# Low bits of two weight pairs on ScalarE, and another order of the first part, in a fused attention and feed-forward kernel

## The chip, the cores and the metric

The kernel runs on one core of a Trainium2 chip. The metric is the device time of one execution in microseconds (us); lower is better. TensorE multiplies matrices, VectorE and ScalarE do elementwise work, POOL (GpSimd) does masks and small powers, and SP issues the DMA transfers from a queue that it takes in order. Each engine takes its own instructions in program order and waits for others by semaphores.

## The reference

Gated linear attention over 4 batches of 8 heads, 768 positions and 48 numbers a head, then a gated feed-forward layer behind an RMS norm, then a second one with squared ReLU:

```python
f = 1 / (1 + exp(-f_logit))
for t in range(S):
    state = f[:, :, t, :, None] * state + einsum('bhd,bhe->bhde', k[:, :, t], v[:, :, t])
    y[:, :, t] = einsum('bhd,bhde->bhe', q[:, :, t], state)
x = y.transpose(0, 2, 1, 3).reshape(B * S, H * D)
...
xn = x / sqrt(mean(x * x) + 1e-6) * rms_g
x = (silu(xn @ w_gate) * (xn @ w_val)) @ w_out          # 384 -> 1536 -> 384
...
out = relu(x @ w_in) ** 2 @ w_out2                      # 384 -> 2048 -> 384
```

The weights come as 64-bit floats; the rest is 32-bit.

## The kernel before

**Units and groups.** Attention is cut into 24 units: 6 chunks of 128 positions by 4 batches. Unit `u` is chunk `u // 4` of batch `u % 4`. Four units form a group of 512 rows for the first feed-forward layer; there are six groups. A group runs twelve steps: `G` and `V` are the gate and value products of step `f` (nine matmuls of 512 columns each, since every 32-bit operand is split in a high and a low part), `si` is the silu of the gate on ScalarE, `vs` the product with the value on VectorE, `hh` and `hl` split the result in high and low, and `O` multiplies it into three accumulator banks. `G` has one PSUM bank and `V` one, so the next `G` waits for the silu of the last, and the next `V` for its product.

**Weights.** The first layer's weights come in 18 pairs (`g0 v0`, `o0 g1`, `v1 o1`, ...) of 768 64-bit numbers a partition, tile `raw` with two 32-bit words for each number. A pair is made 32-bit in pieces: `wl` loads it; `ws` takes the high word as a float and scales it (ScalarE, line 568); `wb` shifts the result by 3 bits (VectorE, line 572) and ors the low word's top 3 bits in (line 579); `wc` ors the sign in (line 589); `wh` and `wz` split the number in a high part (ScalarE, line 626) and a low one (VectorE, line 630). `raw` and `m` have two buffers each, so a later load waits for an earlier pair.

**The first part.** Everything up to the end of group 0 is written out by hand in the string `FIRST`. Each word is a piece and its index, and the pieces are issued in that order; every engine's own order follows from it. `lr`, `lf`, `lk`, `lq`, `lv` load parts of a unit 0 to 3, and `ld` loads all of a later unit (gates `ff`, then `qk`, then `v`). `gr` and `gf` are the sigmoids of the gates (for units from 4 on `gr` is both, lines 296 and 297), `sb` and `sa` the scans, `mk` and `mq` the products with `k` and `q`, `sc` the scores, `ca` and `cb` the copies of the scores out of PSUM, `pa` and `pb` the masks on POOL, `kt` and `kc` the transposed keys, `y` the attention, `kv` and `st` the state, `no`, `pw`, `nr` the norm, `xt`, `xh`, `xl` the input tiles of the first layer. `du` issues dummy matmuls. `G0` needs `xl` of units 0 to 3.

**The seam.** The last word of group 0's work is `O11`. It also copies the three accumulators out of PSUM (ScalarE, line 936) and has SP store each (line 937). Then the loop `phase1` begins with group 1, whose pieces are placed by a planner. Its first segment has, on ScalarE and in this order, the gates of unit 8, a small copy of their end (which waits for VectorE's scan of them) and the silu of group 1's step 0. From there to the end the order doesn't depend on `FIRST`.

Of the kernel before, what the change touches and what calls it, by code (L numbers as in the profile page):

```python
# [8 lines left out]
F32 = mybir.dt.float32  # L9
F32R = mybir.dt.float32r  # L10
BF16 = mybir.dt.bfloat16
I32 = mybir.dt.int32
AF = mybir.ActivationFunctionType
ALU = mybir.AluOpType
PSUM = bass.MemoryType.PSUM

P = 128
# [12 lines left out]


FIRST = """
lr1 lr3 gr1 lf1 lr0 gf1 sb1 gr0 lk1 lf0 lq0 gf0 lq1 sa1 mk1 lr2 sb0 mq1 gr2 lk0 wl3 lf2 gr3 kt1 sa0 lk2 sc1 lv1
kc1 cb1 ca1 ws3 pa1 lf3 lv0 mk0 mq0 sb2 gf2 sc0 wb3 sa2 ca0 mk2 pb1 y1 pa0 ld4 kv1 cb0 sb3 lq2 pb0 gf3 no1 kt0
kc0 y0 wc3 lk3 st1 no0 sa3 mk3 kt2 pw1 kv0 pw0 nr1 xt1 wl0 mq2 gr4 lq3 lv2 st0 wh3 nr0 kc2 du6 sc2 lv3 ws0 xh1
sb4 wl1 mq3 sc3 cb2 wz3 pb2 ca2 wb0 cb3 pa2 ca3 pb3 sa4 xl1 ld5 xt0 wc0 xh0 kv2 y2 xl0 du10 kt3 mk4 ws1 no2 wh0
wl2 pa3 y3 pw2 nr2 no3 wb1 kc3 xt2 kv3 mq4 st2 pw3 nr3 xt3 xh2 xh3 wz0 ws2 wc1 xl2 xl3 sc4 wh1 en0 wl4 kt4 gr5
G0 si0 wb2 wz1 wc2 wh2 cb4 V0 sb5 wz2 ws4 pb4 vs0 G1 st3 en4 de4 wb4 si1 ca4 hh0 mk5 pa4 kc4 V1 wc4 sa5 wl8 hl0
G2 y4 ws8 vs1 wh4 wl5 kt5 no4 kv4 wz4 si2 wb8 O0 G3 mq5 wc8 pw4 hh1 ws5 wh8 en3 wb5 V2 wc5 wl6 st4 nr4 wh5 wz8
hl1 vs2 ws6 wl7 wz5 ld6 sc5 wb6 si3 kc5 ws7 O1 hh2 wc6 ca5 V3 cb5 wh6 hl2 pa5 wb7 gr6 pb5 wz6 wc7 xt4 wl9 O2 kv5  # L40
sb6 vs3 de5 G4 ws9 wb9 si4 wh7 xh4 y5 V4 wl10 wz7 hh3 G5 wc9 hl3 ws10 en1 no5 vs4 wb10 mk6 de6 pw5 wc10 wh9 O3
en5 wl11 si5 hh4 wz9 hl4 ld7 nr5 sa6 V5 ws11 vs5 wl12 xl4 G6 si6 wb11 wh10 wz10 V6 wc11 vs6 hh5 ws12 wb12 en6
wh11 wz11 wl15 wc12 wh12 kt6 st5 hl5 ws15 O4 G7 hh6 V7 gr7 si7 mq6 O5 wl13 wz12 hl6 wb15 kc6 sc6 mb6 O6 xt5 ws13
vs7 wc15 wh15 G8 wb13 hh7 en2 sb7 wz15 si8 hl7 wl14 xh5 wc13 V8 ma6 ws14 vs8 wh13 wl16 G10 y6 wb14 sa7 wc14 V10
no6 si10 wz13 wl17 O7 hh8 pw6 wh14 wz14 xl5 G9 mk7 mq7 nr6 xt6 ws16 vs10 sc7 hl8 ma7 mb7 V9 xh6 kv6 si9 de7 wb16
y7 vs9 ws17 wc16 O8 hh9 wh16 xl6 hl9 en7 no7 kt7 kc7 wb17 wz16 O9 pw7 wc17 nr7 ld8 st6 wh17 xt7 hh10 xh7 G11
wz17 hl10 V11 si11 O10 xl7 vs11 hh11 kv7 hl11 st7 O11
"""


def exact_path(tc, qk, ff, vT, rms_g, out, w1_order, w2_order, raw_load, to_f32, f64):
# [9 lines left out]
    with ExitStack() as st:  # L61
# [12 lines left out]
        with tc.For_i(0, B, 1) as b, tc.For_i(0, NPAIR, 1) as a, tc.For_i(0, D // EG, 1) as g:  # L74
            bs, as_, gs = bass.ds(b, 1), bass.ds(a, 1), bass.ds(g, 1)

            def load(src, nm):
                t = sp.tile([P, NCH, C], F32, tag=nm, name=nm)
                nc.sync.dma_start(t, src.rearrange("o u p c t -> (o u p) c t"))
                return t.rearrange("p c t -> p (c t)")  # L80

            qt, kt = load(qkb[bs, as_, 0], "xq"), load(qkb[bs, as_, 2], "xk")
            ft = load(fb[bs, as_, 0, :, :, 1:], "xf")
            nc.scalar.activation(ft, ft, AF.Sigmoid)
            fr = cp.tile([P, EG, S], F32, name="x_fr")
# [28 lines left out]
    with ExitStack() as st:  # L114
# [25 lines left out]
        with tc.For_i(0, B * NCH, 1) as i:  # L140
# [3 lines left out]
            rs = sp.tile([P, 1], F32, tag="zrs", name="zrs")  # L144
            nc.scalar.activation(sq, x, AF.Square, accum_out=rs)
            nc.gpsimd.tensor_scalar(rs, rs, 1.0 / DM, EPS, op0=ALU.mult, op1=ALU.add)
# [17 lines left out]
            for f in range(F1):  # L164
                gp, vp = proj(("g", f), xt, "zg"), proj(("v", f), xt, "zv")
                h = sp.tile([P, C], F32, tag="zh", name=f"zh{f}")
                nc.scalar.activation(h, gp, AF.Sigmoid)
                nc.vector.tensor_mul(h, h, gp)
# [9 lines left out]
            for f in range(F2):  # L178
                hp = proj(("a", f), x3, "zg" if f % 2 else "zv")
                r = sp.tile([P, C], F32, tag="zh", name=f"zr{f}")  # L180
                nc.scalar.activation(r, hp, AF.Relu)
                nc.vector.tensor_mul(r, r, r)
# [7 lines left out]
def tile_linear_attention_moe(  # L190
# [11 lines left out]
    nc = tc.nc  # L202
# [4 lines left out]
    def pool(name, stack=main, **kw):  # L207
        return stack.enter_context(tc.tile_pool(name=name, **kw))

    ps = pool("ps", bufs=1, space=PSUM)  # L210
    cp = pool("const", bufs=1)
# [16 lines left out]
    seed = cp.tile([P, NPAIR, C + 1], F32, name="seed")  # L228
    neghalf = cp.tile([P, 1], F32, name="neghalf")
    half = cp.tile([P, 1], F32, name="half")  # L230
    epsT = cp.tile([P, 1], F32, name="epsT")
    ends = cp.tile([P, NCH * B, NPAIR], F32, name="ends")
    gT = cp.tile([P, KT], F32, name="gT")
# [3 lines left out]
    def constants():  # L237
        nc.gpsimd.memset(half, 0.5)
        nc.gpsimd.memset(mask, 1.0)
        nc.gpsimd.affine_select(  # L240
            out=mask, in_=mask, compare_op=ALU.is_ge, fill=0.0,
            base=-(C - 1), pattern=[[1, C]], channel_multiplier=1,
        )
        nc.gpsimd.memset(floor, A_MIN)
        nc.gpsimd.memset(floor[:, :, 0:1], 1.0)
        nc.gpsimd.memset(seed, 0.0)
        make_identity(nc, ident)
        nc.gpsimd.memset(neghalf, -0.5)
        nc.gpsimd.memset(epsT, EPS)
        for st in state:  # L250
            nc.gpsimd.memset(st, 0.0)
# [43 lines left out]
    def sig(x):  # L295
        nc.scalar.activation(x, x, AF.Tanh, scale=0.5)
        nc.scalar.activation(x, x, AF.Identity, bias=half, scale=0.5)

# [255 lines left out]
    f64 = w1.dtype != F32  # L554
    raws = {}

    def raw_load(pool, pair):
        src = w1[w1_order.index(pair)] if pair in w1_order else w2[w2_order.index(pair)]
        if f64:
            raw = pool.tile([P, 2 * DM, 2], I32, tag="raw", name="raw")  # L560
            nc.sync.dma_start(raw.rearrange("p a b -> p (a b)"), src.bitcast(I32))
        else:
# [7 lines left out]
    def to_f32_shift(m, raw):  # L570
        mi = m.bitcast(I32)
        nc.vector.tensor_scalar(
            mi, mi, 3, 0x7FFFFFF8,
            op0=ALU.logical_shift_left, op1=ALU.bitwise_and,
        )

    def to_f32_or(m, raw):
        mi = m.bitcast(I32)
        nc.vector.scalar_tensor_tensor(
            mi, raw[:, :, 0], 29, mi, op0=ALU.logical_shift_right, op1=ALU.bitwise_or,  # L580
        )

    def to_f32_low(m, raw):
        to_f32_shift(m, raw)
        to_f32_or(m, raw)

    def to_f32_sign(m, raw):
        mi = m.bitcast(I32)
        nc.vector.scalar_tensor_tensor(
            mi, raw[:, :, 1], -2 ** 31, mi, op0=ALU.bitwise_and, op1=ALU.bitwise_or,  # L590
        )

    def to_f32_bits(m, raw):
        to_f32_low(m, raw)
        to_f32_sign(m, raw)
# [8 lines left out]
    def wscale(pair):  # L604
        if f64:
            m = rp.tile([P, 2 * DM], F32, tag="m", name="m", bufs=2)
            to_f32_scale(m, raws[pair][0])
            raws[pair][1] = m

    def wbits_low(pair):  # L610
        if f64:
            to_f32_low(raws[pair][1], raws[pair][0])

    def wbits_sign(pair):
        if f64:
            to_f32_sign(raws[pair][1], raws[pair][0])

    def whigh(pair):
# [15 lines left out]
    def w2_half(key):  # L634
        n, f = key
        e = DM * (2 if f64 else 1)
        o = "ab".index(n) * e
        src = w2[f].bitcast(I32) if f64 else w2[f]
        return src[:, o:o + e]
# [104 lines left out]
    wz = mask.bitcast(BF16)  # L744
# [8 lines left out]
    def prologue():  # L753
        nc.sync.dma_start(gT, rms_g.rearrange("(k p) -> p k", p=P))
        for u in range(UG):
            unit_tiles(u)
        constants()
        dense(12)
# [200 lines left out]
    def piece(kind, i):  # L959
# [21 lines left out]
        ld=load_unit, sb=scan_b, en=keep_end, sa=scan_a, mk=mul_k, mq=mul_q, sc=scores, kt=ktrans, kc=kcopy,  # L981
        y=attend, kv=kv, de=decay, st=state_add, no=norm, pw=power, nr=norm2, xt=xtrans, xh=xhigh, xl=xlow,
    )
    pair_piece = dict(wl=wload, ws=wscale, wb=wbits_low, wc=wbits_sign, wh=whigh, wz=wlow)

    def step_piece(kind, gi, f):
        nm = f"{gi}_{f}"
# [467 lines left out]
```

## Time and profile before

| | |
|---|---|
| time, median of 3 runs | 934.64 us (934.61 to 936.6) |
| time of the profiled execution | 936.63 us |
| its span, first to last instruction | 934.8 us |
| mean granted clock of TensorE | 0.993 |
| busy: TensorE, VectorE, ScalarE, POOL | 98%, 68%, 52%, 4% |

A time is that of the whole execution; the span leaves out what lies around the first and the last instruction. Starts in the profile count from the span's start. TensorE is the fullest engine by far, so a change elsewhere counts only where TensorE waits for it.

### The profile page before, as it was taken

What the parts mean: (1) busy time and instruction counts of PE and PEld (TensorE: products, weight loads), DVE (VectorE), ACT (ScalarE), POOL (GpSimd) and SP (SyncE); (2) the same over time, 40 slices, a digit from 0 to 9 for tenths busy, and PEclk for the clock granted to TensorE, in tenths of its full rate; (3) what the DMA queues carried; (4) which work ended last, traced back from release to release, by engine and by line L of the source; (5) the groups of instructions that cost most, each with busy time, mean ns of one, the idle gap of its engine ahead of it and who ended that gap; (6) DMA issues with size and microseconds to landing.
All of it is one profiled execution on the core that took longest, in us unless ns stands there. A gap on an engine that the chain in (4) does not pass through costs nothing.

```text
span 934.8 us, 15751 instructions
## 1 busy us (share of the span) xinstructions
PE 913.7 (98%) x5945; PEld 809.2 (87%) x5945; DVE 640.2 (68%) x1147; ACT 488.4 (52%) x1020; POOL 33.6 (4%) x54
## 2 busy tenths in 40 slices
PE   6799999999999999999999999999999999999997
PEld 4578877888888888888888889999999999999997
DVE  7899967777667776676565727756766676666552
ACT  6876655445544544455343525465546554645551
POOL 3210000000000000000000000000000000000000
PEclk8999999999999999999999999999999999999999
DMA  9455525548636745535444649530754075315300
GB/s 336 165 207 198 179 81 195 161 135 242 205 127 195 234 130 178 190 122 176 132 144 150 215 167 318 171 128 18 231 168 127 21 239 161 121 34 178 119 26 29
DMA packets 78387, 148.48 MB, mean 159 GB/s; under 512 B 17248, under 2 KB 44000, under 8 KB 78304
## 3 DMA queue, kind: packets, MB, share of 16 engines
q1 hardware_dynamic: 78304, 147.39, 48.7%
q8 instruction: 49, 0.80, 0.4%
q14 instruction: 34, 0.28, 0.1%
HBM read 115.12 MB, written 32.24 MB: 158 GB/s over the span
## 4 chain that ended last, share of the span: by engine, by line
PE 89%; ACT 3%; DMA 3%; DVE 2%; SPq 1%; issue 1%; POOL 1%; ACTq 0%; DVEq 0%; POOLq 0%
PE o L741 7%; PE o L739 7%; PE o L740 7%; PE X L1131 7%; PE Y L1131 6%; PE g L739 5%; PE v L739 5%; PE acc L739 5%; PE v L741 5%; PE acc L741 5%; PE v L740 5%; PE acc L740 5%; PE g L741 5%; PE g L740 5%; PE T L1131 2%; PE R L1131 2%
## 5 line engine op out<-in xcount | busy, mean ns | idle before, releaser
L741 PE MATMUL o<-wb,h 128*128 128x384 f32 x384 | 128.6, 335 | 0.0
L740 PE MATMUL o<-wb,h 128*128 128x384 f32 x384 | 128.3, 334 | 0.0
L739 PE MATMUL o<-wb,h 128*128 128x384 f32 x384 | 128.3, 334 | 0.0
L1001 ACT CAST hh<-sg 128x512 fp32r<-128x512 f32 x72 | 44.7, 620 | 111.5 <-DVE sg L998 111.4
L998 DVE TENSOR_TENSOR sg<-v,sg 128x512 f32<-128x512 f32 x72 | 49.5, 687 | 58.5 <-PE v L741 57.3
L1131 PE MATMUL X<-xc,wa 128*128 128x384 f32 x360 | 82.4, 336 | 0.0
L993 ACT ACTIVATE sg<-g 128x512 f32<-128x512 f32 x72 | 42.8, 594 | 74.3 <-PE g L741 74.0
L741 PEld LDWEIGHTS o<-wb,h 128*128 128x128 f32 x384 | 72.1, 188 | 0.5
L739 PEld LDWEIGHTS o<-wb,h 128*128 128x128 f32 x384 | 72.1, 188 | 0.0
L740 PEld LDWEIGHTS o<-wb,h 128*128 128x128 f32 x384 | 72.1, 188 | 0.0
L1131 PE MATMUL Y<-xc,wa 128*128 128x384 f32 x300 | 68.3, 335 | 0.0
L1131 PEld LDWEIGHTS X<-xc,wa 128*128 128x128 f32 x360 | 63.8, 188 | 1.8 <-ACT d L1206 1.2
L1210 DVE TENSOR_TENSOR c<-T,c 128x384 f32<-128x384 f32 x40 | 22.3, 557 | 51.9 <-PE T L1131 42.7
L1131 PEld LDWEIGHTS Y<-xc,wa 128*128 128x128 f32 x300 | 53.3, 188 | 0.7 <-DVE c L1210 0.6
L1003 DVE TENSOR_TENSOR hl<-sg,hh 128x512 fp32r<-128x512 f32 x72 | 48.9, 679 | 5.4 <-ACT hh L1001 5.3
L1161 DVE TENSOR_TENSOR h<-d,h 128x384 fp32r<-128x384 f32 x60 | 32.8, 554 | 26.2 <-ACT h L1160 26.0
L1160 ACT CAST h<-d 128x384 fp32r<-128x384 f32 x60 | 30.2, 511 | 34.4 <-PE o L741 34.4
L1206 ACT COPY d<-X 128x384 f32<-128x384 f32 x40 | 19.1, 478 | 54.7 <-PE X L1131 54.7
L739 PE MATMUL g<-xh,wh_o 128*128 128x512 f32 x108 | 43.3, 401 | 1.5 <-ACT sg L993 1.5
L739 PE MATMUL g<-xh,wh_g 128*128 128x512 f32 x108 | 43.4, 402 | 0.0
L739 PE MATMUL v<-xh,wh_v 128*128 128x512 f32 x108 | 42.5, 393 | 0.7 <-DVE state L503 0.6
L739 PE MATMUL v<-xh,wh_g 128*128 128x512 f32 x108 | 42.8, 396 | 0.0
(195 smaller groups left out, 2234.5 us busy)
## 6 DMA issues: line engine op xcount, KB each, us to landing
wa<-w2d_c SPq DMA_DIRECT2D x100, 384.0 KB, 3.4
raw<-in_w_dram SPq DMA_DIRECT2D x18, 768.0 KB, 4.4
ff<-in_ff_dram SPq DMA_DIRECT2D x20, 516.0 KB, 4.4
qk<-in_qk_dram SPq DMA_DIRECT2D x20, 512.0 KB, 6.4
w2d_c<-ws_c SPq DMA_DIRECT2D x50, 192.0 KB, 2.8
raw_a<-in_w_dram SPq DMA_DIRECT2D x22, 384.0 KB, 4.3
wb<-w2d_b SPq DMA_DIRECT2D x16, 384.0 KB, 3.6
v<-in_vp_dram SPq DMA_DIRECT2D x24, 192.0 KB, 5.3
```

The lines of the kernel that those rows point to most:

```text
L739: nc.tensor.matmul(o, lh, rh, start=first, stop=False)
L740: nc.tensor.matmul(o, lh, rl, start=False, stop=False)
L741: nc.tensor.matmul(o, ll, rh, start=False, stop=last)
L993: nc.scalar.activation(dd["s", f], dd["g", f], AF.Silu)
L998: nc.vector.tensor_mul(dd["s", f], dd["v", f], dd["s", f])
L1001: nc.scalar.copy(dd["h", f][0], dd["s", f])
L1003: nc.vector.tensor_sub(dd["h", f][1], dd["s", f], dd["h", f][0].bitcast(F32))
L1131: nc.tensor.matmul(o, w[a], x[:, b], start=first and n == 0, stop=last and n == 2, skip_group_check=True,)
L1160: nc.scalar.copy(t[:, 0], r)
L1161: later(lambda: nc.vector.tensor_sub(t[:, 1], r, t[:, 0].bitcast(F32)))
L1206: nc.scalar.copy(t, bk[b])
L1210: nc.vector.tensor_add(t, bk[b], t)
```

## The change

Pairs 3 (`g2 v2`) and 5 (`v3 o3`) get a new piece `wt`. ScalarE reads the upper 16 bits of the low word as an unsigned number, scales it by 2^-13 and adds a bias just under a half below, so that the rounding to an integer leaves the top 3 bits; it writes them over the low word. VectorE then ors the sign to these bits (`sign_and_low`) and in a second pass shifts `m` and ors the two (`shift_and_join`). For these two pairs the shift as a pass of its own is gone. The string `FIRST` is a different order of the same pieces; its dummy matmuls are 5 and 6 in place of 6 and 10.

```diff
     neghalf = cp.tile([P, 1], F32, name="neghalf")
+    under = cp.tile([P, 1], F32, name="under")
...
+        nc.gpsimd.memset(under, 2.0 ** -14 - 0.5)
...
+    def low_bits(raw):
+        top = raw.bitcast(U16)[:, :, 1]
+        nc.scalar.activation(raw[:, :, 0], top, AF.Identity, bias=under, scale=2.0 ** -13)
+
+    def sign_and_low(raw):
+        nc.vector.scalar_tensor_tensor(
+            raw[:, :, 0], raw[:, :, 1], -2 ** 31, raw[:, :, 0], op0=ALU.bitwise_and, op1=ALU.bitwise_or,
+        )
+
+    def shift_and_join(m, raw):
+        mi = m.bitcast(I32)
+        nc.vector.scalar_tensor_tensor(
+            mi, mi, 3, raw[:, :, 0], op0=ALU.logical_shift_left, op1=ALU.bitwise_or,
+        )
...
+    floored = set()
+
+    def wlow_bits(pair):
+        if f64:
+            low_bits(raws[pair][0])
+            floored.add(pair)
+
     def wbits_low(pair):
-        if f64:
+        if pair in floored:
+            sign_and_low(raws[pair][0])
+        elif f64:
             to_f32_low(raws[pair][1], raws[pair][0])
 
     def wbits_sign(pair):
-        if f64:
+        if pair in floored:
+            shift_and_join(raws[pair][1], raws[pair][0])
+        elif f64:
             to_f32_sign(raws[pair][1], raws[pair][0])
...
-wz17 hl10 V11 si11 O10 xl7 vs11 hh11 kv7 hl11 st7 O11
...
+pw7 V11 vs11 O10 nr7 xt7 hh11 kv7 hl11 xh7 st7 O11 ld8 xl7
```

The first lines show how the program's order moves. Names carry the unit or step and, behind the last underscore, a buffer number; line numbers of the changed kernel are a little larger.

ScalarE near the start of its work, where pair 3 is converted, before:

```order
L348 COPY sm1_True_200<-sc1_1_188 128x512
L348 COPY sm1_False_202<-sc1_0_187 128x512
L568 ACTIVATE m_204<-raw_176 128x768
L304 ACTIVATE f2_118<-f2_118 128x4x128
L348 COPY sm0_False_227<-sc0_0_214 128x512
L348 COPY sm0_True_264<-sc0_1_215 128x512
L304 ACTIVATE f3_123<-f3_123 128x4x128
```

and in the changed kernel:

```order
L351 COPY sm1_True_199<-sc1_1_190 128x512
L351 COPY sm1_False_203<-sc1_0_189 128x512
L588 ACTIVATE raw_171<-raw_171,under_93 128x768
L571 ACTIVATE m_230<-raw_171 128x768
L307 ACTIVATE r3_125<-r3_125 128x4x128
L307 ACTIVATE f2_119<-f2_119 128x4x128
L351 COPY sm0_True_264<-sc0_1_215 128x512
L351 COPY sm0_False_267<-sc0_0_214 128x512
L307 ACTIVATE f3_124<-f3_124 128x4x128
```

`low_bits` (line 588) comes ahead of the scale of pair 3, and unit 3's sigmoid `r3`, which was earlier in the queue, stands behind them.

ScalarE around the silu of group 0's first step (`sg_0_0`), before:

```order
L626 CAST wh_o0_554<-m_465 128x768
L312 COPY ends_94<-r0_109 128x4
L296 ACTIVATE ff5_406<-ff5_406 128x8x128
L297 ACTIVATE ff5_406<-ff5_406,half_92 128x8x128
L993 ACT_TABLE_LOAD
L993 ACTIVATE sg_0_0_577<-g_0_0_567 128x512
```

and in the changed kernel:

```order
L571 ACTIVATE m_551<-raw_494 128x768
L452 COPY ktok4_562<-ktp4_553 128x512
L571 ACTIVATE m_566<-raw_523 128x768
L351 COPY sm4_False_568<-sc4_0_538 128x512
L1022 ACT_TABLE_LOAD
L1022 ACTIVATE sg_0_0_590<-g_0_0_570 128x512
L655 CAST wh_v1_595<-m_551 128x768
L299 ACTIVATE ff5_451<-ff5_451 128x8x128
L300 ACTIVATE ff5_451<-ff5_451,half_92 128x8x128
```

Unit 5's gates moved from ahead of the silu to behind it; a key copy, a second scale (pair 4) and a mask copy of unit 4 stand ahead of it in their place.

SP's queue at the end of group 0 (`x3o` are the copies of the accumulators, `ff8`, `qk8` and `v8` unit 8's tiles, `gB` and `raw_a` loads of `phase1`), before:

```order
L561 DMA raw_1266<-in_w1_dram 128x1536
L277 DMA ff8_1430<-in_ff_dram 128x1032
L278 DMA qk8_1429<-in_qk_dram 128x1024
L279 DMA v8_1431<-in_vp_dram 128x384
L937 DMA x3d_0_81<-x3o_0_0_1511 128x512
L937 DMA x3d_0_81<-x3o_0_1_1514 128x512
L937 DMA x3d_0_81<-x3o_0_2_1517 128x512
L1019 DMA gB_96<-in_rms_g_dram 128x384
L651 DMA raw_a0_1536<-in_w2_dram 128x768 x2
```

and in the changed kernel:

```order
L564 DMA raw_1301<-in_w1_dram 128x1536
L966 DMA x3d_0_81<-x3o_0_0_1499 128x512
L966 DMA x3d_0_81<-x3o_0_1_1502 128x512
L966 DMA x3d_0_81<-x3o_0_2_1505 128x512
L280 DMA ff8_1509<-in_ff_dram 128x1032
L281 DMA qk8_1508<-in_qk_dram 128x1024
L282 DMA v8_1510<-in_vp_dram 128x384
L1048 DMA gB_97<-in_rms_g_dram 128x384
L680 DMA raw_a0_1533<-in_w2_dram 128x768 x2
```

Unit 8's three loads moved from ahead of the three stores to behind them.

## Rows read from the trace of the kernel before

**Rows 1.** The page: busy time, share of the span and instructions of each engine.

```profile
PE 913.7 (98%) x5945; PEld 809.2 (87%) x5945; DVE 640.2 (68%) x1147; ACT 488.4 (52%) x1020; POOL 33.6 (4%) x54
```

**Rows 2.** Windows of two stages: length; busy PE, PEld, DVE, ACT, POOL; clock; DMA share, GB/s.

```profile
12.79:46.37 33.58, 25.26 (x318) 18.49 (x318) 29.20 (x45) 28.62 (x62) 11.40 (x12) 0.93 0.64 236
48.60:133.36 84.76, 84.69 (x626) 68.80 (x626) 78.32 (x117) 56.74 (x115) 6.59 (x7) 1.00 0.46 157
```

**Rows 3.** TensorE's waits after 41 us: total, times, longest.

```profile
PE g L739 <- ACT sg L993: 1.5, 2, 0.8
```

**Rows 4.** TensorE in order of time: start, length, idle before and its releaser.

```profile
10.67 2.08 PE L341 MATMUL sc<-q,k 64*128 64x128 f32 x16 [0.85 <-DVE q L322]
...
29.98 0.67 PE L472 MATMUL y<-v,sm_False 128*64 128x48 f32 x16 [1.99 <-POOL sm_False L353]
...
31.05 4.02 PE L749 MATMUL du<-mask 128*128 128x512 bf16 x10
...
46.42 0.50 PE L739 MATMUL g<-xh,wh_o 128*128 128x512 f32 x1 [0.77 <-ACT sg L993]
```

**Rows 5.** ScalarE in order of time, up to the first silu.

```profile
12.79 0.58 ACT L348 COPY sm_True<-sc 128x512 f32<-128x512 f32 x1 [0.33 <-PE sc L341]
...
13.75 0.92 ACT L568 ACTIVATE m<-raw 128x768 f32<-128x768 f32 x1
14.57 0.62 ACT L304 ACTIVATE f<-f 128x512 f32<-128x512 f32 x1
...
19.34 0.49 ACT L510 ACTIVATE xn<-y 128x384 f32<-128x384 f32 x1 [0.57 <-PE y L472]
...
31.16 0.49 ACT L510 ACTIVATE xn<-y 128x384 f32<-128x384 f32 x1 [0.75 <-PE y L472]
...
33.24 0.58 ACT L519 ACTIVATE xn<-y,rs 128x384 f32<-128x384 f32 x1 [0.44 <-POOL rs L516]
36.62 0.49 ACT L510 ACTIVATE xn<-y 128x384 f32<-128x384 f32 x1 [2.80 <-PE y L472]
```

**Rows 6.** ScalarE and TensorE in order of time, around the seam.

```profile
132.19 1.96 ACT L936 COPY x3o<-acc 128x512 f32<-128x512 f32 x3 [2.01 <-PE acc L741]
134.05 1.06 ACT L296 ACTIVATE ff<-ff 128x1024 f32<-128x1024 f32 x1
135.14 1.15 ACT L297 ACTIVATE ff<-ff,half 128x1024 f32<-128x1024 f32 x1
...
137.69 0.59 ACT L993 ACTIVATE sg<-g 128x512 f32<-128x512 f32 x1
...
133.36 0.39 PE L739 MATMUL g<-xh,wh_g 128*128 128x512 f32 x1
...
138.34 0.50 PE L739 MATMUL g<-xh,wh_o 128*128 128x512 f32 x1 [0.73 <-ACT sg L993]
```

**Rows 7.** VectorE's shift, grouped by line, 48.6 to 133.4 us: busy, mean ns, idle.

```profile
L572 DVE TENSOR_SCALAR m<-m 128x768 int32<-128x768 int32 x14 | 8.2, 583 | 0.0
```

**Rows 8.** SP's issues in order of time: unit 8's gates, and the seam.

```profile
109.47 0.42 SPq L277 DMA_DIRECT2D ff<-in_ff_dram  x1
...
132.80 1.69 SPq L937 DMA_DIRECT2D x3d<-x3o  x3
134.54 0.45 SPq L1019 DMA_DIRECT2D gB<-in_rms_g_dram  x1
```

**Rows 9.** Gate loads, issue to landing (us): at 109.47, then lines 284 and 277.

```profile
ff<-in_ff_dram SPq DMA_DIRECT2D x1, 516.0 KB, 5.3
...
DMA to landing us min/median/max: 3.5/4.0/8.1
...
DMA to landing us min/median/max: 3.7/6.6/7.0
```

**Rows 10.** Windows over the two spells of a lower clock; PEclk is the granted clock.

```profile
7.54:14.37 6.83, 4.59 (x32) 3.95 (x34) 6.64 (x10) 4.07 (x8) 0.44 (x1) 0.50 1.03 396
31.43:34.85 3.42, 3.42 (x10) 1.29 (x8) 3.39 (x8) 1.92 (x5) 1.37 (x2) 0.50 0.71 223
```

## What the change should do to the time

> **What bounds the kernel now.** I read the page first: TensorE is busy for 98% of the span, so the time is TensorE's fixed work plus the stretches in which it stands still [rows 1]. The windows by stage then show where these are. In the first part, up to the second gate product, ScalarE is busy for 28.62 of 33.58 us and TensorE for 25.26; after it TensorE is busy for 84.69 of 84.76 us, up to the seam where group 1 begins [rows 2]. TensorE's own list of waits after 41 us is led by two on ScalarE's silu, 1.5 us in total [rows 3]. The change touches the order of the first part alone, so three places carry the prediction: when the second gate product (`G1`) starts, whether TensorE stays fed until the seam, and what the seam costs.
>
> **The first part.** `G1` needs the bank that ScalarE's silu of `G0` empties, and it started at 46.42 [rows 4]. So I add up ScalarE from its first mask copy at 12.79 to that silu. Of the 33.58 us, four waits take 0.57 + 0.75 + 0.44 + 2.80 = 4.56 us [rows 5]; 29.0 us are left for work (the window counts 28.62 as busy, the rest are small gaps). The longest wait is for the last unit's attention, `y3`, which stands on TensorE behind ten dummy matmuls of 4.02 us [rows 4].
>
> In the new order the same stretch of ScalarE's queue holds one more conversion scale (0.92 long, 0.82 from its start to the next one's), the new operation of pair 3 (bounded below), one more sigmoid (0.62) and two more copies of 512 (0.58), which I take 0.1 shorter as well, for they overlap alike [rows 5]. It no longer holds unit 5's gates, which moved behind the silu (passes like those of 1.06 and 1.15, 2.3 with the gaps [rows 6]), nor a small copy (0.1). The new operation reads 768 numbers of 16 bits and adds a bias. No row has that; the scale of 768 without a bias takes 0.92 and the biased one of 1,024 takes 1.15 [rows 5, 6], so I take 0.9, with twice that as the bound for strided 16-bit reads. Net: 0.8 + 0.9 + 0.5 + 0.5 + 0.5 - 2.4 = +0.8, so 29.8 us of work.
>
> It starts earlier. The first mask copy follows the first scores (16 matmuls, 2.08 us at 10.67 [rows 4]), which waited for VectorE's `q1`; before, a scan and its reciprocal of another unit stood between `k1` and `q1`, and now they stand behind it. The scores can then begin when the transposes end, about 0.9 us earlier. So the copy is at about 11.9 and the silu ends at 11.9 + 29.8 = 41.7 if ScalarE never waits: `G1` 4.7 us earlier. I don't expect that. The ten dummies are gone from in front of `y3` (five stand there, six behind it), so the 2.80 goes, but the shorter waits for POOL's masks and for TensorE should come again in part. With 1.0 us of waits I take **-3.7 us**. Bounds: -4.7, and -0.1 if all 4.56 stay.
>
> The Trainium skill ("ScalarE: Activation LUTs", Rules for kernel authors) would leave adds and multiplies to VectorE, and its price for an ACTIVATE with a pointer bias gives an estimate of 0.92 us for 768 elements. By it the move costs the path about 0.9 in pair 3, which the sum above holds already from rows; here ScalarE has the fuller queue, so the trace bears that advice out for pair 3.
>
> On VectorE each of the two pairs loses the shift (0.58 [rows 7]); its other two passes stay as long as they were. In pair 3 that frees VectorE where ScalarE sets the pace; nothing is counted. Pair 5's new operation on ScalarE lies in the next stretch, where ScalarE is busy for 56.74 of 84.76 us [rows 2]; without that cover it would cost 0.9.
>
> **The stretch that TensorE fills.** Before and after, the same twelve steps and units 4 to 7 follow. VectorE was busy there for 78.32 of 84.76 us [rows 2], close enough that an order could starve TensorE. Over the whole stretch it has 6.4 us to spare and, with pair 5's shift gone, 7.0. Place by place I added, in each order, VectorE's pieces up to the weights that a product needs, and TensorE's up to that product, at the durations of the trace: the closest place had some 0.2 us to spare before, and has 0.3 now. I take **0**, bounds 0 and +1.
>
> **The seam.** Here the order of a load changes. Unit 8's gates (`ld8`) were loaded at 109.47, long before ScalarE wanted them at 134.05 [rows 6, 8]. Now `ld8` is behind `O11`, and SP takes its queue in order: the three stores of group 0's result come first, each waiting for ScalarE's copy of a bank that `O11` fills. The stores held SP from 132.80 to 134.49, and the next issue was at 134.54 [rows 8]. Group 1's first product began at E = 133.36 [rows 6], so unit 8's load is issued at E + 1.2. It lands 5.3 us after issue in the nearest row, a gate load with a load ahead and `qk` right behind it; the 15 later gate loads took 3.5 at least and 4.0 in the median, the five of this first part 3.7 to 7.0 [rows 9]. I take 5.0. Queued behind the gates on ScalarE are the silu of group 1's first step, and on VectorE, behind the scan, its product. From the gates' start to the next gate product of TensorE took 134.05 to 138.34, 4.29 us [rows 6]: two passes, the scan on VectorE, the small copy, the silu. So that product starts at E + 1.2 + 5.0 + 4.3 = E + 10.5, where it was E + 4.98: **+5.5 us**. Bounds by landing in 3.5 and 7.0: +4.0 and +7.5. TensorE has two products to cover it, 138.34 - 0.73 - 133.36 = 4.25 us, and stands still for 6.3 us where it stood 0.73.
>
> **The clock.** After that stillness TensorE should be at half speed for a while. The clock rows show it twice, at 1.2 GHz: from 31.43 to 34.85, soon after a wait of 1.99 us, and from 7.54 to 14.37, 3.4 and 6.8 us [rows 4, 10]. A spell costs half of the work done in it: 1.7 us for the short one if all of it is work, 0.3 if most falls into the wait, 3.4 for the long one. I take **+1.7**.
>
> **Sum.** -3.7 + 0 + 5.5 + 1.7 = +3.5 us. The profiled execution had a span of 934.8 [rows 1] in a time of 936.63, so 1.8 lie around it: 938.3 and 940.1. The median of the three runs shown is 2.0 lower, 934.64, and against it the sum is 938.1.
>
> **Rivals.** *Quick landing* (18%): the load lands like the fastest lone gate load, 3.5 us, and the clock costs 1.0: -3.7 + 4.0 + 1.0 = +1.3, 935.9; with ScalarE waiting for nothing, 934.9. For it: SP's queue holds nothing but stores ahead of the load. Against it: `qk` and `v` of unit 8 follow at once, and the row with that neighbourhood has 5.3. The Trainium skill ("DMA: Bandwidth & Descriptors", Anatomy of one DMA) gives 2.0 us plus the bytes at 436 GB/s; by that 516 KB land in 3.2 us, an estimate, and the sum would be +1.7 with the clock as taken. No row here is that short.
>
> *The first part gains little* (10%): the waits come back at other places, ScalarE being the fuller queue with one more operation of up to 1.8 us; -0.1 in place of -3.7 gives +7.1, 941.7.
>
> *The late load costs nothing* (7%): then the first part's gain stands alone, -3.7, 930.9. It decides at one point: the gates must be in SBUF when ScalarE has copied `O11`'s last bank, E + 0.8. With the issue behind the stores at E + 1.2 this can't be, unless SP doesn't keep that order or the silu doesn't stand behind the gates; each 1 us that they land beyond that costs 1 us.
>
> *The edit doesn't do what it says* would be a 16-bit pass at 1.8 us: +0.9, inside the forecast's range.
>
> **How the numbers follow.** The forecast has 63%, its own range +0.9 to +6.0 (935.5 to 940.6); 2% are left for what I don't see. Within 0.2%, about what a measurement of this kernel can tell from no change, is 932.8 to 936.5. Same: the quick landing and the lowest seventh of the forecast, 0.27. Slower: the rest of the forecast and the first part that gains little, 0.65. Faster: the load that costs nothing, 0.08. The range starts at the quick landing with the full gain and the least of the clock (-4.7 + 4.0 + 0.3 = -0.4, 934.2), less 0.8 because the runs shown lie up to 2.0 apart, and ends at the top of the forecast's own, 940.5; it leaves out 7% below and some 10% above.
>
> **What would show it.** In the new profile: `G1` near 42.7, with ScalarE's 2.80 us wait before the last norm gone; VectorE without the shift in pairs 3 and 5, and a new ScalarE row of 0.8 to 1.0 us; no wait of TensorE over 0.3 us between `G1` and the seam; unit 8's gate load issued after the three stores; a wait of ScalarE for that DMA of about 5 us, a wait of TensorE for the silu of 5.5 to 7, and the granted clock at 0.5 behind it. Wrong would be: the gate load ahead of the stores, a landing under 4 us, or `G1` after 45.

## The result, and the profile after

The changed kernel took 943.05 us in the median of 10 runs (938.23 to 945.88), the kernel before 936.23 us in 10 runs on the same chip (934.61 to 936.87). The ratio is 1.0066, interval 1.0054 to 1.0079: 6.2 us slower by the ratio and 6.8 between the medians, where the sum said 3.5. The profiled execution took 941.82 us, with a span of 939.7 us and a mean granted clock of 0.988 (0.993 before).

TensorE is busy 3.5 us longer than in [rows 1], for 5 instructions fewer. The page's line of busy times:

```profile
PE 917.2 (98%) x5940; PEld 814.2 (87%) x5940; DVE 640.3 (68%) x1145; ACT 490.6 (52%) x1022; POOL 33.8 (4%) x55
```

TensorE's waits after 38 us (total, times, longest) have one large entry in place of the 1.5 us of [rows 3]:

```profile
PE g L768 <- ACT sg L1022: 5.0, 1, 5.0
PE v L768 <- DVE state L506: 0.4, 1, 0.4
```

That wait is at the seam. ScalarE, SP and TensorE in order of time there, to be read against [rows 6, 8]:

```profile
131.38 1.98 ACT L965 COPY x3o<-acc 128x512 f32<-128x512 f32 x3 [0.52 <-PE acc L770]
137.53 1.06 ACT L299 ACTIVATE ff<-ff 128x1024 f32<-128x1024 f32 x1 [4.18 <-DMA ff<-in_ff_dram]
138.62 1.15 ACT L300 ACTIVATE ff<-ff,half 128x1024 f32<-128x1024 f32 x1
...
141.17 0.59 ACT L1022 ACTIVATE sg<-g 128x512 f32<-128x512 f32 x1
```

```profile
131.99 1.71 SPq L966 DMA_DIRECT2D x3d<-x3o  x3
133.75 0.45 SPq L280 DMA_DIRECT2D ff<-in_ff_dram  x1
```

```profile
46.14 0.39 PE L768 MATMUL g<-xh,wh_o 128*128 128x512 f32 x1
...
132.57 0.40 PE L768 MATMUL g<-xh,wh_g 128*128 128x512 f32 x1
...
141.81 0.79 PE L768 MATMUL g<-xh,wh_o 128*128 128x512 f32 x1 [4.99 <-ACT sg L1022]
...
150.76 0.39 PE L768 MATMUL g<-xh,wh_g 128*128 128x512 f32 x1
```

The first of these rows is `G1`; group 1's first product is at E = 132.57. SP issues unit 8's gates behind the three stores, at E + 1.18; they land 3.78 us later, when ScalarE's wait of 4.18 us ends; from there to the product of the next step it is 4.28 us: E + 9.24, where it was E + 4.98 [rows 6]. That is **+4.26 us**.

The first part, on ScalarE, to be read against [rows 5]. The first rows are the first mask copy and pair 3's new operation, the following ones all its waits up to the silu:

```profile
11.91 0.59 ACT L351 COPY sm_True<-sc 128x512 f32<-128x512 f32 x1 [0.84 <-PE sc L344]
...
12.87 1.01 ACT L588 ACTIVATE raw<-raw,under 128x768 int32<-128x768 uint16 x1
13.76 0.91 ACT L571 ACTIVATE m<-raw 128x768 f32<-128x768 f32 x1
...
15.95 0.59 ACT L351 COPY sm_True<-sc 128x512 f32<-128x512 f32 x1 [0.24 <-PE sc L344]
...
18.50 0.59 ACT L452 COPY ktok<-ktp 128x512 f32<-128x512 f32 x1 [0.94 <-PE kv L490]
...
23.28 0.58 ACT L522 ACTIVATE xn<-y,rs 128x384 f32<-128x384 f32 x1 [0.22 <-POOL rs L519]
...
28.91 0.59 ACT L351 COPY sm_False<-sc 128x512 f32<-128x512 f32 x1 [1.13 <-PE sc L344]
...
36.93 0.58 ACT L522 ACTIVATE xn<-y,rs 128x384 f32<-128x384 f32 x1 [0.76 <-POOL rs L519]
...
41.95 0.59 ACT L452 COPY ktok<-ktp 128x512 f32<-128x512 f32 x1 [0.72 <-PE ktp L375]
...
45.14 0.60 ACT L1022 ACTIVATE sg<-g 128x512 f32<-128x512 f32 x1
```

The copy stands where it was forecast, the work is 45.14 - 11.91 - 4.01 = 29.2 us up to the silu, and the six waits make 4.01 us, nearly the 4.56 of before. So the silu came 0.63 us earlier (45.77 before) and `G1` at 46.14, 0.28 earlier than in [rows 4].

Four windows around spells of a lower clock (length; busy PE, PEld, DVE, ACT, POOL; clock; DMA):

```profile
8.60:18.75 10.15, 8.80 (x88) 7.42 (x88) 9.72 (x12) 7.39 (x13) 3.82 (x4) 0.51 1.04 397
25.66:29.10 3.44, 3.44 (x37) 2.81 (x35) 2.81 (x6) 2.31 (x7) 1.67 (x2) 0.55 0.90 361
39.00:42.40 3.40, 3.40 (x20) 3.08 (x21) 2.81 (x7) 2.68 (x6) 0.00 (x0) 0.50 0.03 8
141.60:145.00 3.40, 3.19 (x8) 2.57 (x9) 3.21 (x5) 1.70 (x3) 0.00 (x0) 0.53 1.03 416
```

Three spells now lie in the first part and one behind the seam, where two lay before [rows 10]. The account of the two profiled executions: E is 0.79 us earlier, the seam costs +4.26, and from the delayed product to the end it takes 797.89 us in place of 796.46, +1.43; the sum, +4.90, is the difference of the spans. The ten runs lost more than that.

### The profile page after: what moved, and what is told of

The parts are those of the page before. It is cut to its first block, busy times and chain, and to the rows that moved or that the text cites. A ratio compares the mean times of both kernels' runs of the same rounds, so it can differ in the third digit from the quotient of the medians.

```text
span 939.7 us, 15743 instructions
## 1 busy us (share of the span) xinstructions
PE 917.2 (98%) x5940; PEld 814.2 (87%) x5940; DVE 640.3 (68%) x1145; ACT 490.6 (52%) x1022; POOL 33.8 (4%) x55
## 4 chain that ended last, share of the span: by engine, by line
PE 84%; DVE 6%; DMA 2%; issue 1%; ACT 1%; SPq 0%; POOL 0%; ACTq 0%; POOLq 0%
PE o L770 7%; PE o L768 7%; PE o L769 7%; PE X L1160 7%; PE Y L1160 6%; PE g L768 5%; PE v L768 4%; PE acc L768 4%; PE acc L769 4%; PE v L770 4%; PE v L769 4%; PE acc L770 4%; PE g L769 4%; PE g L770 4%; PE T L1160 2%; PE R L1160 2%
## 5 line engine op out<-in xcount | busy, mean ns | idle before, releaser
L770 PE MATMUL g<-xh,wl_o 128*128 128x512 f32 x108 | 42.6, 395 | 0.0
```

Of the source, the lines that this page charges most:

```text
L770: nc.tensor.matmul(o, ll, rh, start=False, stop=last)
```

## The experiments

All ratios are to the kernel before, run on the same chip; the runs lie on several chips, where its medians were 935.6 to 936.8 us, so a ratio is not the quotient of two medians of this table. *Silu* is the start of the first silu on ScalarE; *E to next G* the seam as above; *rest* is from that product to the end of the span; *half clock* is the time at 1.2 GHz, summed over half-microsecond windows of the trace, up to 50 us and behind the seam. These columns are of the one profiled execution of each.

| kernel | median us (runs) | ratio, interval | silu | E to next G | rest | half clock |
|---|---|---|---|---|---|---|
| before | 936.23 (10) | 1 | 45.77 | 4.98 | 796.5 | 10.2, 0 |
| changed | 943.05 (10) | 1.0066 [1.0054, 1.0079] | 45.14 | 9.24 | 797.9 | 17.1, 3.4 |
| load_early | 936.35 (11) | 0.9997 [0.9988, 1.0005] | 42.13 | 4.97 | 795.8 | 10.2, 0 |
| before_load_late | 942.45 (5) | 1.0061 [1.0048, 1.0074] | 44.69 | 9.33 | 799.0 | 10.2, 6.8 |
| bits_alone | 936.32 (11) | 0.9999 [0.9990, 1.0008] | 45.22 | 4.98 | 795.7 | 13.7, 0 |
| order_alone | 942.56 (6) | 1.0056 [1.0034, 1.0078] | 44.95 | 9.21 | 799.4 | 20.5, 6.8 |
| warm_all | 933.89 (8) | 0.9972 [0.9959, 0.9984] | 43.00 | 4.97 | 795.6 | 3.4, 0 |
| warm_start | 935.19 (12) | 0.9984 [0.9972, 0.9996] | 46.01 | 4.97 | 795.7 | 13.7, 0 |
| no_dummies | 935.28 (12) | 0.9989 [0.9979, 1.0000] | 43.19 | 4.98 | 796.9 | 17.1, 0 |
| seam_dummies | 940.38 (12) | 1.0024 [1.0011, 1.0038] | 45.63 | 9.31 | 795.3 | 20.5, 0 |
| before_warm | 935.39 (11) | 1.0001 [0.9992, 1.0010] | 45.51 | 4.97 | 795.3 | 3.4, 0 |
| after_warm | 940.25 (5) | 1.0046 [1.0033, 1.0060] | 43.34 | 9.42 | 796.8 | 10.2, 3.4 |
| warm_no_bits | 934.12 (11) | 0.9979 [0.9970, 0.9988] | 44.59 | 4.98 | 796.7 | 6.8, 0 |

**Taking the change apart.** The theory was that the late load costs what the change loses; the rival was that the order or the new operation does. Four kernels, each one or two words away from the kernel before or the changed one:

*load_early*, the changed kernel with the load ahead again:

```diff
-hl11 xh7 st7 O11 ld8 xl7
+hl11 xh7 st7 ld8 O11 xl7
```

> The changed kernel with one word moved: unit 8's load (ld8) stands ahead of O11, so SP issues it before the stores. Theory (the late load costs the wait at the seam and the half clock behind it, 4.3 + 1.4 us in the profile after): the wait of TensorE for the silu at the seam falls from 5.0 to under 1 us, the clock there stays at 1.0, and the time falls by 5 to 7 us against the changed kernel, to within 1.5 us of the kernel before. Rival (the new order of the first part itself costs the time): the time falls by less than 2 us.

It fell back to the time of before, but not below. Its profiled execution was the fastest of its 11 runs (932.69 us) and had the whole gain of the first part that was forecast, `G1` at 42.78; the median had nothing of it.

*before_load_late*, the kernel before with that word moved the other way:

```diff
-pw7 wc17 nr7 ld8 st6 wh17 xt7
+pw7 wc17 nr7 st6 wh17 xt7
...
-kv7 hl11 st7 O11
+kv7 hl11 st7 O11 ld8
```

> The kernel before with the one word ld8 moved behind O11, nothing else. Theory of the late load: 5 to 7.5 us slower than before, with a wait of 4 to 6 us of TensorE for the silu at the seam. Rival (the load's place doesn't matter, the order around it does): within 1 us of before.

The one word makes the old kernel as slow as the changed one, 1.0061, with the same wait on TensorE (the delayed product and the gate product of the step behind it, in order of time):

```profile
141.64 0.80 PE L738 MATMUL g<-xh,wh_o 128*128 128x512 f32 x1 [5.09 <-ACT sg L992]
...
151.29 0.40 PE L738 MATMUL g<-xh,wh_g 128*128 128x512 f32 x1
```

*bits_alone*, the old order with the new pieces ahead of the scales of pairs 3 and 5:

```diff
-kc1 cb1 ca1 ws3 pa1
+kc1 cb1 ca1 wt3 ws3 pa1
...
-wc8 pw4 hh1 ws5 wh8
+wc8 pw4 hh1 wt5 ws5 wh8
```

> The order of before with the new low-bits piece put ahead of the scale in pairs 3 and 5. Theory (ScalarE sets the first part's pace at pair 3, VectorE the pace elsewhere): the new ScalarE row takes 0.9 to 1.0 us, VectorE loses two shifts of 0.55, and the time is within 1 us of before. Rival (the passes on 16-bit numbers or the in-place writes cost): 2 us or more slower.

Nothing: 0.9999, within 0.1%.

*order_alone*, the changed order without them:

```diff
-kt0 sc0 lq3 wt3 lv0 pa1
+kt0 sc0 lq3 lv0 pa1
...
-wc8 hl1 ws5 wt5 mk5
+wc8 hl1 ws5 mk5
```

> The changed kernel's order without the low-bits piece (pairs 3 and 5 converted as before). Theory: the order carries the loss, so it is as slow as the changed kernel within 1.5 us, 5 to 8 us slower than before. Rival (the new piece carries part of the loss): 2 us or more faster than the changed kernel.

1.0056, all of the loss as far as its wide interval tells; the six runs lie between 938.8 and 944.8 us. The order holds one thing more than other places: half of unit 5's mask moved from ScalarE and POOL to VectorE (`mb5` for `cb5` and `pb5`), and half of unit 7's the other way (`ca7` and `pa7` for `ma7`). So the loss hangs on the place of `ld8` in either order (1.0066 and 1.0056 against 0.9997; 1.0061 against 1), and neither the rest of the order nor the operation shows in a median.

**Why the first part's gain is missing.** The theory here was half clock: TensorE's small products take nearly twice as long at 1.2 GHz, and ScalarE, which in the new order has fewer other reasons to wait, waits for them. TensorE in order of time, the scores of the first units, first in the changed kernel, then in *load_early*:

```profile
9.76 2.08 PE L344 MATMUL sc<-q,k 64*128 64x128 f32 x16
13.80 2.08 PE L344 MATMUL sc<-q,k 64*128 64x128 f32 x16 [0.17 <-DVE q L325]
23.91 1.16 PE L344 MATMUL sc<-q,k 64*128 64x128 f32 x16 [2.05 <-ACT xn L522]
26.80 2.08 PE L344 MATMUL sc<-q,k 64*128 64x128 f32 x16
```

```profile
9.85 2.08 PE L343 MATMUL sc<-q,k 64*128 64x128 f32 x16
13.83 2.08 PE L343 MATMUL sc<-q,k 64*128 64x128 f32 x16
23.66 1.16 PE L343 MATMUL sc<-q,k 64*128 64x128 f32 x16 [1.21 <-ACT xn L521]
26.01 1.16 PE L343 MATMUL sc<-q,k 64*128 64x128 f32 x16
```

The same 16 matmuls take 2.08 us or 1.16. Where the spell fell on the scores at 26.8, ScalarE waited 1.13 us for them; in *load_early* they ran at full clock and that wait isn't there: its waits from the first mask copy to the silu are 0.18, 0.53 and 0.33, 1.04 us in all.

*warm_start*, *load_early* with more dummies at the start, and *warm_all*, with more of them later too:

```diff
-        dense(12)
+        dense(24)
```

```diff
-pw0 nr0 ws0 sc2 kc2
+pw0 nr0 ws0 du8 sc2 kc2
...
-kc3 wl2 du6 xt2
+kc3 wl2 du11 xt2
```

> The early-load kernel with 24 dummies at the start in place of 12, nothing else: they fill the time until the first keys. Theory of the half clock: the first scores run at full speed, about 1 us each faster, and 1 to 2 us are won against the early load. Rival (the first scores wait for loads and VectorE, not for the clock): under 0.7 us.

> The early-load kernel with more dummy matmuls where TensorE stands still in the first part: 24 in place of 12 at the start, 8 new ones ahead of unit 2's scores, 11 in place of 6 behind y3. Theory (the new order's gain in the first part is lost where TensorE's small matmuls run at half speed and ScalarE waits for them): the clock is at 1.0 through most of the first part, ScalarE waits for scores, keys and kv by 2 us less in all, G1 starts near 43 in the profiled run, and the time is 2 to 4 us below before and below the early load. Rival (the waits come from POOL's masks and powers and from the order itself, whatever the clock): within 1 us of the early load.

*warm_all* is faster than before and than *load_early*, 0.9972, and the intervals of the two don't touch; *warm_start* lies between, its interval overlapping both. ScalarE in *warm_all*, its first mask copy, all its waits up to the silu, and the silu:

```profile
11.47 0.58 ACT L350 COPY sm_True<-sc 128x512 f32<-128x512 f32 x1
...
16.65 0.58 ACT L350 COPY sm_True<-sc 128x512 f32<-128x512 f32 x1 [1.29 <-PE sc L343]
...
19.09 0.58 ACT L451 COPY ktok<-ktp 128x512 f32<-128x512 f32 x1 [0.84 <-PE kv L489]
...
23.90 0.58 ACT L521 ACTIVATE xn<-y,rs 128x384 f32<-128x384 f32 x1 [0.26 <-POOL rs L518]
...
43.00 0.60 ACT L1021 ACTIVATE sg<-g 128x512 f32<-128x512 f32 x1
```

2.39 us of waits, all before 24 us: 11.47 + 29.2 + 2.39 = 43.06. That sum, start plus 29.2 plus waits, also gives the silu of *load_early*: 12.01 + 29.2 + 1.04 = 42.25, for 42.13.

*no_dummies*, *load_early* without `du5` and `du6`, was to show the opposite:

> The early-load kernel without the 5 and 6 dummy matmuls of the first part (the 12 at the start stay). Theory of the half clock: more of the first part at half speed, the mean granted clock lower, 1 to 4 us slower than the early load. Rival (the dummies don't matter, or cost TensorE time on the path): the same within 0.7 us or faster.

It missed: 0.9989, not slower at all, though its trace has 17.1 us at half clock. Its third spell, 32.5 to 40, fell on little that ScalarE waited for (0.25 and 0.57 us). So the amount of half clock alone doesn't set the time; it counts where it meets a product that ScalarE waits for, and dummies do not always move that. What TensorE saved by the eleven dummies left out is not separated from this.

*before_warm*, the old order with `dense(24)`:

> The kernel before with 24 in place of 12 dummy matmuls at its start, nothing else. Theory (the small products of the first part run at half clock in either order, and longer work at the start shortens that): 1 to 2 us less than before, as the same edit gave 1.2 us with the changed order, so 934.5 to 936 against a before of about 936.5, and a spell at half clock that is shorter or later than 7.5 to 14.4 us. Rival (only the changed order has small products where the clock is low, and the old order hides them behind its ten dummies and ScalarE's work): no difference, within 0.5 us.

The rival held: 1.0001. In its trace the clock is 1.00 from 10 to 30 us, and ScalarE still waits 0.74, 0.72, 0.45 and 2.77 us, as in [rows 5]; the silu is at 45.51. The window (columns as above) and the longest wait:

```profile
10.00:30.00 20.00, 11.97 (x204) 9.48 (x206) 19.83 (x28) 18.45 (x39) 9.35 (x9) 1.00 0.95 368
...
36.36 0.49 ACT L510 ACTIVATE xn<-y 128x384 f32<-128x384 f32 x1 [2.77 <-PE y L472]
```

The old order has these waits at either clock, so half clock there costs it nothing that shows. The profiled execution was the warmest of the 11, though, with a mean granted clock of 0.997; the others had 0.991 to 0.995, where the kernel before had 0.991 to 0.993 on the same chip, so the median by itself says little.

The runs without a trace say more, for each has its mean granted clock on record. In *load_early* the three at 0.993 or more took 932.7 to 934.9 us, the eight at 0.988 to 0.991 took 935.5 to 937.3. In *warm_start* the five at 0.995 or more took 933.0 to 934.7, the seven at 0.990 to 0.994 took 935.0 to 937.8. In the old order the time doesn't go with the clock: *before_warm* took 935.3 us at 0.997, and 934.8 and 935.3 at 0.991. This is how the runs fall and not an edit, but it says the same as the traces: the new order loses by half clock, and the old one doesn't as far as these runs show.

*warm_no_bits*, *warm_all* without `wt3` and `wt5`:

> The best kernel so far (load of unit 8 ahead of O11, more dummies in the first part) without the two pieces wt3 and wt5: VectorE shifts the low words of pairs 3 and 5 itself again. Theory (with the first part warm, ScalarE sets its pace, and the 0.89 us of low_bits in pair 3 lie on that path): 0.5 to 0.9 us less than with them, a ratio of 0.996 to 0.997 to before. Rival (VectorE's freed 0.58 us is worth as much, or TensorE's small products still set the pace): within 0.4 us of 0.9972.

0.9979 against 0.9972: the 0.5 to 0.9 us that were expected did not come, and there is no difference that these intervals tell; they leave over 1 us either way. The profiled execution had ScalarE wait 2.18 us for scores that stood on TensorE behind the eight added dummies, a wait that *warm_all* doesn't have, so this pair doesn't give the price of the piece alone.

**The half clock behind the seam.** *seam_dummies*, the changed kernel with 20 dummies behind group 1's first value product, in the time in which TensorE stands still:

```diff
                 step_piece("V", gi, f)
+                if gi == 1 and f == 0:
+                    dense(20, ps.tile([P, 2, 2 * C], F32, tag="pa", name="dus"))
```

> The changed kernel, its late load kept, with 20 dummy matmuls on TensorE behind the value product of group 1's first step, in the time in which it waits for the silu. Theory (the seam costs a wait of about 4.3 us beyond before's and a spell at half clock of about 1.5): the wait stays, the clock behind it stays at 1.0, and the time falls by 1 to 2.5 us against the changed kernel. Rival (the wait is all of it): within 0.7 us of the changed kernel.

1.0024 in place of 1.0066: 3.9 us less by the ratios, where 1 to 2.5 were expected; the two intervals allow 1.5 to 6.4. TensorE in order of time:

```profile
137.94 4.49 PE L778 MATMUL dus<-mask 128*128 128x512 bf16 x20
...
143.15 0.50 PE L768 MATMUL g<-xh,wh_o 128*128 128x512 f32 x1 [0.73 <-ACT sg L1022]
...
150.77 0.39 PE L768 MATMUL g<-xh,wh_g 128*128 128x512 f32 x1
```

The product is as late as ever (E + 9.31), but the matmul takes 0.50 us and not 0.79, no spell follows, and the rest takes 795.3 us. What a spell costs is read from this product to the gate product of the step behind it, between which TensorE does the same work in every kernel. It takes 7.62 us here (150.77 - 143.15) and 7.6 in all nine traces without a spell; 8.95 in the changed kernel and 9.11 in *after_warm*, with a spell of 3.4 us; 9.65 in *before_load_late* and 9.77 in *order_alone*, with one of 6.8 us. So a short spell costs 1.4 to 1.5 us and a long one 2.1 to 2.2: the long ones began over 2 us ahead of the product, in the wait. The column *rest* is a blunter measure: it is 795.3 to 796.9 without a spell, 796.8 and 797.9 with a short one, 799.0 and 799.4 with a long one, and so holds 1 us and more of other differences.

The 12 runs of *seam_dummies* lie in two groups, four at 936.6 to 937.2 us and seven at 940.3 to 941.0, with one between. The mean granted clock was 0.996 in the four and 0.988 to 0.992 in the seven; the profiled one is of the upper group, with 20.5 us at half clock in its first part.

*after_warm*, the changed kernel, load late, with the dummies of *warm_all*:

> The changed kernel, with unit 8's load behind O11 as it is there, and the 24 dummies at the start, 8 more ahead of unit 2's scores and 11 in place of 6 ahead of unit 2's input tile. Theory (the late load and the cold first part are two separate costs that add up): the 2.3 us that this edit gave with the early load come off again, so about 940.5, ratio to before 1.004 to 1.005, with the seam's wait still at 5.0 us. Rival (the runs differ by the clock all through, so that a warmer first part also spares the spell behind the seam): under 939, ratio under 1.003.

1.0046, as the sum of two separate costs would have it; the seam stays at E + 9.42 and the rival is out.

## Why the prediction was wrong

The direction was right and its main cause was the one named; the time lay above the range. Two of the three things that it called signs of being wrong came: the landing took under 4 us and `G1` started after 45. The step that failed is in the first part: "With 1.0 us of waits I take **-3.7 us**." Step by step:

- **First part, mis-sized, -3.7 forecast, 0.** The start of ScalarE's stretch (11.9 forecast, 11.91 measured), its work (29.8, 29.2 + 0.6) and the new operation (0.9; 0.89 from its start to the next, 1.01 long) were right. The 2.80 us wait went, as forecast. The waits were not: 4.01 us in place of 1.0, 3.0 of them on TensorE's small products at half clock, a price that the sum didn't have. `G1` came 0.28 us earlier, not 3.7. The bound of -0.1 held this case; the value was taken near the other end on the argument that waits come again "in part", with no row for which. In medians the load ahead of `O11` leaves 0.9997, so the gain isn't there typically; the profiled execution of *load_early* had it, and with more dummies (*warm_all*) 2.6 us of it are there by the ratio.
- **Steady stretch, right.** 0 forecast; from `G1` to E no wait of TensorE over 0.4 us.
- **Seam, right in mechanism, +5.5 forecast, +4.26 measured.** The issue at E + 1.2 (1.18) and the 4.29 us behind the gates (4.28) held; the landing was taken as 5.0 us from one row with a load ahead, and took 3.78 (3.75 to 3.95 in the five traces with a late load). The rows allowed 3.5 to 7.0 [rows 9]. The Trainium skill ("DMA: Bandwidth & Descriptors", Anatomy of one DMA) gave 3.2 as an estimate, nearer than my value but still short of the measured 3.78; its fit is for transfers that GpSimd issues, and SP issued this one.
- **Clock behind the seam, +1.7 forecast, 1.4 in the profiled execution.** The mechanism is shown by *seam_dummies*. The size varies: in *before_load_late* and *order_alone* the spell was 6.8 us and cost 2.1 and 2.2, under the 3.4 of the bound, because part of it fell in the wait.
- **The sum.** With what was measured it is 0 + 4.3 + 1.4 (or 2.2) = 5.7 (or 6.5), and the kernel lost 6.2 by the ratio. The rival "the first part gains little" is what came, at a smaller price of the seam.

What stays open: why the clock's spells fall where they do from one execution to the next. Only one execution of each kernel has a trace; that the median of the changed kernel has a longer spell behind the seam than the profiled execution is inferred from the two other kernels, from the mean granted clock of its six slowest runs (0.985 to 0.988) and from the gain of *seam_dummies*. Of that gain 1.7 us (3.9 less the 2.2) have no account; the intervals are wider than that, and with two groups 4 us apart the ratio depends on how many runs fell in each. That half clock takes the first part's gain rests on traces of one execution each, on *warm_all* and on how the runs fall.

## What to carry to other kernels

A load that moves behind stores in an in-order DMA queue inherits their waits: add the store's release, the landing and everything behind the consumer, and compare with the work in hand. Where a gain is to come from waits that vanish, list which wait comes next and at which clock its producer runs; the sum of work alone is only the best case. Before giving up an order that gains nothing, undo its parts one by one: here one word cost 6 us, and the rest, with the load back and TensorE kept busy, beats the kernel before by 2.6 us.

## What the runs showed of the hardware

- Spells at 1.2 GHz lasted from 3.4 to 10.2 us in the 13 traces (0 to 100 and 130 to 160 us). They began at other times in each execution of nearly the same program, and in the new order the times of one kernel went with the mean granted clock: the 10 runs of the changed kernel span 7.7 us, with 0.993 in the fastest and 0.985 to 0.988 in the six slowest. The Trainium skill ("TensorE: Matmul & The Clock Gate", Part 1) says that the number of cold matmuls at the start varies between runs of one kernel; these traces agree, and show the same of spells much later.
- The amount of half clock alone doesn't give its cost: 17.1 us of it in *no_dummies* went with a silu at 43.19, 13.7 us in *warm_start* with 46.01 (its slowest run).
- A wait of 5 us of TensorE, filled with 20 matmuls of 512 columns (4.49 us), left the next product where it was and at full clock, 0.50 us in place of 0.79.
- A ScalarE pass that reads 768 16-bit numbers of every second word and writes 32-bit integers took 1.01 us, 0.1 longer than the 32-bit scale of the same count.
